# A gated MLP after linear attention on one core: a shorter reciprocal root, whole normalisation groups on GpSimd, and a new static instruction order

## Chip, core and metric

One core of a Trainium2 chip runs the whole program. The metric is device time in microseconds (us) of one execution, the median over several.

## The reference, cut to what matters

Linear attention with degree-2 sketched features, then a gated MLP whose gate mixes along the sequence (B=4, H=4, S=1088, D=32, r=8, d_ff=1024):

```python
phi = lambda x: outer(S1 @ x, S2 @ x)              # 8 x 8 = 64 features a head
x = (phi(q) @ (phi(k).T @ v)) / (phi(q) @ sum(phi(k)) + 1e-6)
h = gelu_tanh(x @ w_in);  u, v = h[..., :512], h[..., 512:]
v_n = (v - mean(v)) / sqrt(var(v) + 1e-6) * g_ln   # over the 512 columns
v_s = w_sg @ v_n + b_sg                            # 1088 x 1088 along the sequence
out = x + (u * v_s) @ w_out
```

`S1`, `S2`, `w_in` and `w_out` reach the chip as float64 words.

## The kernel before, in words

The sequence is cut into NT = 9 tiles of 128 rows and, along the free side, into chunks CH of 420, 420 and 248 columns. All work is a list of 1,839 steps (`add`, `step`), each with an engine, and `ORDER` (line 42) is a fixed permutation of them, written out as numbers: every engine (PE, V = VectorE/DVE, A = ScalarE/ACT, G = GpSimd/POOL, SP = the DMA-issuing queue) runs its own steps strictly in that order, and waits on semaphores for steps of others. PSUM buffers and scratch tiles are handed out along the same order: three `ps` buffers, two `pz`, three `po`.

Batch 0 alone is laid out for a short start. SP issues the loads (`first_loads`, line 434): `s` (the sketches), `k0` and `k1` (two parts of the keys), `win1`, `q0` to `q2`, `v0`, `v1`, the mixing weights `w0` to `w8`. `split64` (line 453) turns float64 words into a high and a low single-precision part in steps numbered 0 to 6, then `hi`, `l1`, `l2`; for names in `ONA` with more than 16 columns steps 2 and 4 run on A. The sketch `s` gives `sk` (line 505) and, on A, the expanded sketches `sab` (line 517). PE then runs `pk0` (key features, L526), `q2_0` (query features, L604), `k2_0` (keys by values, L534), `q3_0` (L581), a transpose `tr` (L598) and nine `pv0` (the gate half of `w_in`, L633 to L635). Each `pv0` tile passes A (`gelu`, L650), V (`bn`, bn_stats) or A (`bn`, a squared sum, L653), and a normalisation: group of tiles 0-1 on V (`norm 0`: `Gate.first` and `Gate.rest`, L294 to L311), tiles 2-5 and 6-8 on G after a `first` of three V instructions (`first 2`, `first 6`; `rest_g`, L316 to L330). The roots are a bit trick for the start value and two refinement steps. Then `v3` applies scale and shift (A, L333, or V, L666), and `part` (L673, L674) splits tiles into `ar` high and low, the stationary operands of the sequence mixing: `z0` (L695 to L699) and the columns of L1258 to L1262.

Meanwhile A rounds the mixing weights (`whi`, L668) and G makes their low parts (`w_lo`, L712); `HOLD` keeps G's pieces 12 and 15 of these behind `norm 0` and `norm 2`, the former by a small copy (L731). V converts `wi0` and `wo`; the last of those conversions (`staging`) frees the memory in which the later `gt`, `u`, `gh`, `gl` tiles lie, so no `u` (L764) of batch 0 can be written before it. The attention of batch 1 (k features L941, L267; `K2` L534; query product L996, then PE L1003) and the sums of weight blocks that batches 1 to 3 use (`combine`, L896 to L906, through HBM) run beside it.

Batches 1 to 3 do their mixing in seven instead of eight block products (`pair`); their normalisation groups are tiles 0-4 and 5-8 (GROUPS), each with `first` on V (line 1056) and `rest_g` on G (line 1057). Instructions marked `port` on G get a wait on the last V step marked `port`.

Of the kernel before, what the change touches and what calls it, by code (L numbers as in the profile page):

```python
# [1378 lines left out]
```

## Time and profile before

| | us |
|---|---|
| median of 3 runs (range) | 324.22 (323.77 to 325.99) |
| the profiled execution, whole | 322.75 |
| its span, first to last instruction | 320.9 |
| PE busy in the span | 309.9 |
| DVE / ACT / POOL busy | 256.0 / 207.5 / 49.3 |

The profiled execution is 1.85 us longer than its span and 1.47 us below the median of the runs. A PE that is called busy has matmuls in flight; an idle stretch of it is a wait.

### The profile page before, as it was taken

To read this page: it belongs to the slowest core of one execution; us is meant where nothing else is said; L and a number is where in the kernel's file an instruction comes from. 1 tells how busy PE (TensorE), PEld (TensorE's weight loads), DVE (VectorE), ACT (ScalarE), POOL (GpSimd) and SP (SyncE) were. 2 spreads that over 40 slices of the span, in tenths; PEclk is the share of its full clock that TensorE was granted. 3 is DMA by queue.
4 is the path that set the end of the run, shared out by engine and by line. 5 is a ranking of instruction groups with operands and counts; after the bars stand their busy time and mean duration, and the time that the engine had idled before them with its cause. 6 is when DMAs were issued, how large, how long until landed. Compare 5 with 4: busy or idle time off the path is not lost.

```text
span 320.9 us, 6428 instructions
## 1 busy us (share of the span) xinstructions
PE 309.9 (97%) x2318; PEld 285.0 (89%) x2318; DVE 256.0 (80%) x561; ACT 207.5 (65%) x491; POOL 49.3 (15%) x126
## 2 busy tenths in 40 slices
PE   5998899999999999999999999999999999999995
PEld 5865889898788998899899999988999999999995
DVE  4878999998988799977865787897976586796574
ACT  4679990766799987375959846358789833432421
POOL 0187792000003400000003300000032100000000
PEclk9799999999999999999999999999999999999999
DMA  7948885754778868973486279840534037205802
GB/s 223 389 132 273 274 274 134 236 164 132 216 211 258 235 195 222 349 217 73 125 254 222 73 165 244 253 133 4 156 117 160 0 110 229 109 29 175 283 0 69
DMA packets 42126, 57.08 MB, mean 178 GB/s; under 512 B 4080, under 2 KB 37104, under 8 KB 42096
## 3 DMA queue, kind: packets, MB, share of 16 engines
q1 hardware_dynamic: 41952, 56.64, 58.3%
q8 instruction: 18, 0.29, 0.4%
q14 instruction: 12, 0.10, 0.1%
q10 hardware_dynamic: 144, 0.05, 0.1%
HBM read 46.73 MB, written 9.95 MB: 177 GB/s over the span
## 4 chain that ended last, share of the span: by engine, by line
PE 78%; DVE 8%; ACT 5%; DMA 5%; issue 2%; SPq 1%; DVEq 0%; ACTq 0%
PE pz L843 15%; PE pz L844 15%; PE pz L845 15%; PE po L795 2%; PE po L796 2%; PE po L797 2%; PE ps L758 2%; PE pz L854 2%; PE ps L759 2%; PE ps L760 2%; PE pz L855 2%; PE ps L1037 2%; PE ps L1039 2%; PE ps L1038 2%; PE ps L1003 2%
## 5 line engine op out<-in xcount | busy, mean ns | idle before, releaser
L843 PE MATMUL pz<-w_h,ar 128*128 128x420 f32 (+1 forms) x288 | 94.0, 326 | 0.0
L844 PE MATMUL pz<-w_h,ar 128*128 128x420 f32 (+1 forms) x288 | 93.2, 324 | 0.0
L845 PE MATMUL pz<-w_l,ar 128*128 128x420 f32 (+1 forms) x288 | 93.0, 323 | 0.0
L843 PEld LDWEIGHTS pz<-w_h,ar 128*128 128x128 f32 x288 | 54.1, 188 | 4.1 <-issue 1.4
L844 PEld LDWEIGHTS pz<-w_h,ar 128*128 128x128 f32 x288 | 54.1, 188 | 1.1
L845 PEld LDWEIGHTS pz<-w_l,ar 128*128 128x128 f32 x288 | 54.2, 188 | 0.6
L818 ACT CAST ar<-vn 128x512 fp32r<-128x512 f32 x40 | 24.4, 619 | 23.4 <-PE pz L845 19.2
L789 ACT CAST gh<-gt 128x420 fp32r<-128x420 f32 (+1 forms) x47 | 23.2, 495 | 20.5 <-DVE gt L788 16.2
L819 DVE TENSOR_TENSOR ar<-vn,ar 128x512 fp32r<-128x512 f32 x40 | 27.3, 684 | 9.1 <-ACT ar L818 8.9
L790 DVE TENSOR_TENSOR gl<-gt,gh 128x420 fp32r<-128x420 f32 (+1 forms) x47 | 24.8, 532 | 12.1 <-ACT gh L789 11.7
L764 ACT ACTIVATE u<-ps 128x420 f32<-128x420 f32 (+1 forms) x48 | 21.9, 468 | 12.9 <-PE ps L760 11.3
L788 DVE TENSOR_TENSOR gt<-gt,u 128x420 f32<-128x420 f32 (+1 forms) x47 | 24.8, 532 | 4.1 <-ACT u L764 3.7
L333 ACT ACTIVATE vn<-vn,st 128x512 f32<-128x512 f32 x33 | 25.1, 807 | 0.0
L712 POOL TENSOR_TENSOR w_l<-w_f,w_h 128x420 fp32r<-128x420 f32 (+1 forms) x21 | 21.4, 1045 | 2.2 <-ACT w_h L668 1.2
L1049 ACT ACTIVATE kp<-vn,st 128x512 bf16<-128x512 f32 x27 | 19.4, 720 | 0.5
L774 DVE SCALAR_TENSOR_TENSOR gt<-pz,g_col,b_bc 128x420 f32<-128x420 f32 (+1 forms) x31 | 17.8, 573 | 1.6 <-PE pz L855 1.3
L1046 ACT ACTIVATE vn<-ps 128x512 f32<-128x512 f32 x27 | 16.0, 595 | 3.1 <-PE ps L1039 2.7
L316 POOL TENSOR_TENSOR st<-st 128x4 f32<-128x4 f32 (+2 forms) x8 | 2.5, 314 | 97.9 <-DVE st L298 97.0
L758 PE MATMUL ps<-x_h,win_h 128*128 128x420 f32 (+1 forms) x48 | 16.0, 332 | 0.0
L760 PE MATMUL ps<-x_l,win_h 128*128 128x420 f32 (+1 forms) x48 | 15.7, 328 | 0.0
L759 PE MATMUL ps<-x_h,win_l 128*128 128x420 f32 (+1 forms) x48 | 15.7, 328 | 0.0
L795 PE MATMUL po<-gh,wout_h 128*128 128x420 f32 (+1 forms) x47 | 15.7, 333 | 0.0
(260 smaller groups left out, 709.0 us busy)
## 6 DMA issues: line engine op xcount, KB each, us to landing
w_h<-td SPq DMA_DIRECT2D x26, 420.0 KB
w_l<-td SPq DMA_DIRECT2D x52, 210.0 KB
td<-tmp SPq DMA_DIRECT2D x16, 315.0 KB
w_f<-in_w SPq DMA_DIRECT2D x9, 544.0 KB
eb<-dq SPq DMA_DIRECT2D x6, 364.0 KB
ea<-dq SPq DMA_DIRECT2D x12, 182.0 KB
vn<-in_k SPq DMA_DIRECT2D x3, 576.0 KB
tmp<-in_w SPq DMA_DIRECT2D x16, 105.0 KB
```

Source lines behind the costliest of these rows:

```text
L333: return A.activation(self.vn(t), self.vn(t), AF.Identity, bias=self.nm[:, t : t + 1], scale=self.rs[:, t : t + 1])
L758: mm(o, lhsT=win_h[:, ws], rhs=xh[:, cs], start=True, stop=False)
L759: mm(o, lhsT=win_l[:, ws], rhs=xh[:, cs], start=False, stop=False)
L760: mm(o, lhsT=win_h[:, ws], rhs=xl[:, cs], start=False, stop=True)
L788: add("V", dv(cw), lambda: V.tensor_mul(gt(k)[:, :cw], gt(k)[:, :cw], utt[plan.got[u]][:, :cw]), r=[u], w=[k], free=[u], port=1)
L789: add("A", ac(cw), lambda: A.copy(ght[plan.got[h]][:, :cw], gt(k)[:, :cw]), r=[k], take={h: "gh"})
L790: add("V", dv(cw), lambda: V.tensor_sub(glt[plan.got[l]][:, :cw], gt(k)[:, :cw], f32(ght[plan.got[h]][:, :cw])), r=[h, k], take={l: "gl"}, ...
L818: add("A", ac(n), lambda: A.copy(dst[:, 0], q()), r=r, w=[key])
L819: add("V", dv(n), lambda: V.tensor_sub(dst[:, 1], q(), f32(dst[:, 0])), r=r, w=[key], port=1)
L843: mm(o, lhsT=ar[e][:, 0, t], rhs=wh, start=first, stop=False, skip_group_check=True)
L844: mm(o, lhsT=ar[e][:, 1, t], rhs=wh, start=False, stop=False, skip_group_check=True)
L845: mm(o, lhsT=ar[e][:, 0, t], rhs=wl, start=False, stop=last, skip_group_check=True)
```

## The change

- **Roots.** `first` makes the start value with two instructions instead of three, one bit trick with a factor -0.5 on the integer view. `rest` (V, used by group 0-1 alone) evaluates a cubic in place of two refinement steps: 12 V instructions become 10.
- **GpSimd from the variance on.** For the groups that G normalises, `first` runs on G too: 3 V instructions become 2 G instructions, in front of `rest_g`. This touches `norm 2`, `norm 6` and six groups of batches 1 to 3.
- **Conversions.** `s` joins `ONA`: its steps 2 and 4 (128x16) go from V to A. `wi1 l1` (128x512, a subtraction) goes from V to G.
- **HOLD** is empty, the copy is gone. The list has 1,830 steps. `KG`, `QG` and `FILL` are empty or zero and add nothing.
- **ORDER** is another permutation. Its starts, decoded by engine (`b1` is batch 1; `w_lo n` the n-th piece):

```
SP  before  k0 s win1 k1 q0 v0 q1 v1 w0 ident q2 w1 w2 ...
    after   s k0 k1 q0 win1 v1 v0 w0 q1 ident q2 (b1 q) w1 w2 w3 win0 ...
PE  before  pk0.0 pk0.2 pk0.1 q2_0.0.0 q2_0.0.1 q2_0.1.0 k2_0 (9) q2_0.1.1 q3_0.0 q2_0.2.0 q3_0.1 ...
    after   pk0.0 pk0.1 q2_0.0.0 pk0.2 q2_0.0.1 k2_0 (9) q2_0.1.0 q2_0.1.1 q3_0.0 q2_0.2.0 q3_0.1 ...
    before  ... pv0.7, b1: Q2.0 Q2.1 K1 K1 K1 K2, z0 tiles 0-1, L1260 ... z0.5, b1: Q2.2 K2 K2
    after   ... pv0.7, b1: K1 Q2.1 K1 K1, z0 tiles 0-1, b1: K2 Q2.2 K2 K2, L1260 ...
A   before  wi1.2 sab(4) kb0 sab(4) ...  whi1 x1 x1 ...  gelu7 mean6 skq bn6 ... bn7 ... bn8 v3.1
    after   s.2 s.4 sab(6) kb0 kb0 sab(1,3) qa1 kb0 wi1.2 sab(1,1) ...  skq whi1 x1 x1 ...
            gelu6 bn6 gelu7 (b1 Q2 copies) v3.1 a0.h kb kb bn7 bn8 kb v3.3
V   before  ... bn0 first2 norm0 v3.0 features(3) first6 a0.l ... L996 of b1 at place 86, 114, 139
    after   ... bn0 norm0 v3.0 (2 of combine) a0.l features(3) ... L996 of b1 at place 73, 110, 133
G   before  wi1.l2 w_lo 0-11 norm2 copy norm6 w_lo 12-20 wi0.l2
    after   wi1.l1 w_lo 0 wi1.l2 w_lo 1-10 norm2 w_lo 11 norm6 w_lo 12-20 wi0.l2
```

The diff, cut to its core:

```diff
+ROOT = (1.0, 0.99999624, 1.49998809, 2.51218104, 4.40140684)
-ONA = ("wi1", "wi0", "wo")
-HOLD = {12:0,15:2}
+ONA = ("s", "wi1", "wi0", "wo")
+HOLD = {}
+LOWG = ("wi1",)
...
-        def first(self, t0, n, summed=True):
+        def first(self, t0, n, summed=True, by=None):
-            V.tensor_scalar(yi, ve.bitcast(I32), 1, None, op0=ALU.logical_shift_right)
-            return V.tensor_scalar(yi, yi, -1.0, float(0x9EF759DF), op0=ALU.mult, op1=ALU.add)
+            return by.tensor_scalar(y.bitcast(I32), ve.bitcast(I32), -0.5, float(0x1EF759DF), op0=ALU.mult, op1=ALU.add)
...
             V.tensor_mul(h, h, ve)
-            V.tensor_scalar(p, h, 1.5, 2.5, op0=ALU.mult, op1=ALU.add)
-            V.tensor_mul(p, p, h)
-            V.scalar_tensor_tensor(y, p, 1.875, y, op0=ALU.add, op1=ALU.mult)
-            V.tensor_mul(h, y, y)
-            V.tensor_mul(h, h, ve)
-            V.scalar_tensor_tensor(self.rs[:, ts], h, 1.5, y, op0=ALU.add, op1=ALU.mult)
+            V.tensor_scalar(h, h, 0.5, None, op0=ALU.add)
+            V.scalar_tensor_tensor(p, h, ROOT[3] / ROOT[4], h, op0=ALU.add, op1=ALU.mult)
+            for c in ROOT[2:0:-1]:
+                V.scalar_tensor_tensor(p, p, c / ROOT[4], h, op0=ALU.add, op1=ALU.mult)
+            V.scalar_tensor_tensor(self.rs[:, ts], p, ROOT[0] / ROOT[4], y, op0=ALU.add, op1=ALU.mult)
...
-        onA = n > 16 and name in ONA
+        onA = name in ONA
...
-        step((name, "l1"), "V", 0.61, lambda: V.tensor_sub(t(), t(), f32(hi)), [(name, "hi"), (name, 5)], port=1)
+        step((name, "l1"), "G" if name in LOWG else "V", 0.61, lambda: (G if name in LOWG else V).tensor_sub(t(), t(), f32(hi)), [(name, "hi"), (name, 5)], port=1)
...
-            step(("first", t0), "V", 0.49, lambda t0=t0, n=n, s=summed: g.first(t0, n, s), bn, port=1)
-            step(("norm", t0), "G", 4.1, lambda t0=t0, n=n, s=summed: g.rest_g(t0, n, s), [("first", t0)])
+            step(("norm", t0), "G", 4.1, lambda t0=t0, n=n, s=summed: (g.first(t0, n, s, G), g.rest_g(t0, n, s))[1], bn)
...
-            add("V", 0.55, lambda t0=t0, n=n: g.first(t0, n), r=mk, w=[nk], port=1)
-            add("G", 3.5, lambda t0=t0, n=n: g.rest_g(t0, n), r=mk, w=[nk])
+            add("G", 3.9, lambda t0=t0, n=n: (g.first(t0, n, by=G), g.rest_g(t0, n))[1], r=mk, w=[nk])
```

## Rows read from the trace of the kernel before

**Rows 1.** Page, the span in 40 slices of 8.02 us: PE busy, granted clock (tenths)
```profile
PE   5998899999999999999999999999999999999995
PEclk9799999999999999999999999999999999999999
```

**Rows 2.** Stretches: length, busy PE, PEld, DVE, ACT, POOL; PEclk, DMA, GB/s
```profile
0.00:4.20 4.20, 3.25 (x28) 3.06 (x28) 1.14 (x12) 1.49 (x2) 0.43 (x6) 1.00 0.46 125
4.20:7.40 3.20, 0.57 (x12) 0.43 (x12) 1.78 (x7) 1.24 (x4) 0.00 (x0) 1.00 0.98 325
7.40:11.30 3.90, 3.90 (x33) 3.60 (x35) 3.80 (x9) 2.76 (x11) 0.00 (x0) 0.56 1.05 384
28.00:34.17 6.17, 3.44 (x70) 2.68 (x68) 5.55 (x26) 6.10 (x22) 3.78 (x16) 1.00 0.75 255
43.20:84.20 41.00, 41.00 (x260) 38.38 (x258) 38.40 (x72) 23.35 (x55) 7.13 (x8) 1.00 0.61 177
86.20:315.90 229.70, 229.66 (x1613) 215.87 (x1609) 179.47 (x380) 149.00 (x358) 18.08 (x68) 1.00 0.55 163
```

**Rows 3.** What PE waited for: us in total, times, longest
```profile
PE ps L526 <- DMA k<-in_k: 1.8, 1, 1.8
PE ps L534 <- DVE st L294: 1.4, 1, 1.4
...
PE ps L1003 <- DVE r L996: 0.6, 1, 0.6
PE ps L976 <- DVE vn L267: 0.5, 1, 0.5
```

**Rows 4.** Timeline of SP, the first loads: start, us, what
```profile
1.18 0.41 SPq L435 DMA_DIRECT2D sg_sraw<-in_s  x1
1.64 0.42 SPq L444 DMA_DIRECT2D sg_wraw_wi<-in_w_in  x1
2.11 0.43 SPq L437 DMA_DIRECT2D k<-in_k  x1
```

**Rows 5.** Timeline of DVE: sketch conversion, and the first normalisation group
```profile
3.33 0.17 DVE L470 TENSOR_SCALAR sp_s_t<-sg_sraw 128x16 int32<-128x16 int32 x1 [2.04 <-DMA sg_sraw<-in_s]
...
28.68 0.14 DVE L296 TENSOR_SCALAR st<-st 128x4 f32<-128x4 f32 x1
...
29.13 0.16 DVE L296 TENSOR_SCALAR st<-st 128x2 f32<-128x2 f32 x1
...
31.33 0.16 DVE L311 SCALAR_TENSOR_TENSOR st<-st 128x2 f32<-128x2 f32 x1
```

**Rows 6.** Timeline of POOL: a 128x512 conversion, first and last of group 2-5
```profile
14.50 1.27 POOL L493 TENSOR_TENSOR win_l<-sp_wi_t,sp_wi_e 128x512 fp32r<-128x512 f32 x1 [13.54 <-DVE sp_wi_t L492]
...
29.30 0.20 POOL L316 TENSOR_TENSOR st<-st 128x4 f32<-128x4 f32 x1 [0.88 <-DVE st L296]
...
32.71 0.20 POOL L330 TENSOR_TENSOR st<-st 128x4 f32<-128x4 f32 x1
```

**Rows 7.** Timeline, PE and ACT: first k2_0, q3_0, v3 and z0
```profile
12.20 2.32 PE L534 MATMUL pz<-sg_vx,vn 128*64 128x64 f32 x72
...
15.30 0.92 PE L581 MATMUL pz<-sg_kvx,vn 128*64 128x66 f32 x24
...
32.32 0.80 ACT L333 ACTIVATE vn<-vn,st 128x512 f32<-128x512 f32 x1
...
34.17 0.38 PE L697 MATMUL po<-w_h,ar 128*128 128x248 f32 x1
```

**Rows 8.** Timeline of DVE: one subtraction without, and one beside, POOL's w_lo
```profile
35.29 0.68 DVE L674 TENSOR_TENSOR ar<-vn,ar 128x512 fp32r<-128x512 f32 x1
...
42.27 1.57 DVE L674 TENSOR_TENSOR ar<-vn,ar 128x512 fp32r<-128x512 f32 x1
```

**Rows 9.** Chain that ended last: end of the staging, and batch 1's last L996
```profile
62.64 0.47 DVE wout_l L493
...
84.43 0.82 DVE r L996
```

More of the change, by code (lines that the diff above doesn't have):

```diff
@@ L32 @@
 WARM = 14
+ROOT = (1.0, 0.99999624, 1.49998809, 2.51218104, 4.40140684)
 LOWS = 7
-ONA = ("wi1", "wi0", "wo")
-HOLD = {12:0,15:2}
+ONA = ("s", "wi1", "wi0", "wo")
+HOLD = {}
 V30 = "VAVAVAAAA"
 STAT = "VVA"
+LOWG = ("wi1",)
+KG = ()
+QG = ()
+FILL = 0
 NORM = "VGG"
@@ L262, in tile_kernel, with features @@
         mm(pst[i % 3][:64, :64], lhsT=kp0[:, :64], rhs=kp0[:, :64], start=True, stop=True)
-    def features(out, a, b):
+    def features(out, a, b, by=None):
         sh = [P, 2, 2, R, R]
-        return V.tensor_tensor(
+        return (by or V).tensor_tensor(
             out.rearrange("t (p h i j) -> t p h i j", p=2, h=2, i=R),
-            a[:, :64].rearrange("t (p x h i) -> t p x h i", p=2, x=2, h=2)[:, :, 0].unsqueeze(4).broadcast_to(sh),
+            (a.rearrange("t (p h i) -> t p h i", p=2, h=2) if by else a[:, :64].rearrange("t (p x h i) -> t p x h i", p=2, x=2, h=2)[:, :, 0]).unsqueeze(4).broadcast_to(sh),
             b.rearrange("t (p h j) -> t p h j", p=2, h=2).unsqueeze(3).broadcast_to(sh),
@@ L288, in vn @@
             return vn[:, t, :DG]
-        def first(self, t0, n, summed=True):
+        def first(self, t0, n, summed=True, by=None):
             ve, y = (x[:, :n] for x in self.ch[t0][:2])
-            yi, ts = y.bitcast(I32), slice(t0, t0 + n)
+            ts, f = slice(t0, t0 + n), -0.5 if by is G else -0.5 / ROOT[4] ** 2
+            by = by or V
             if summed:
-                V.tensor_scalar(ve, self.mv[:, ts, 1], -0.5 / DG, -0.5 * EPS, op0=ALU.mult, op1=ALU.add)
+                by.tensor_scalar(ve, self.mv[:, ts, 1], f / DG, f * EPS, op0=ALU.mult, op1=ALU.add)
             else:
-                V.tensor_scalar(ve, self.mv[:, ts, 1], EPS, -0.5, op0=ALU.add, op1=ALU.mult)
-            V.tensor_scalar(yi, ve.bitcast(I32), 1, None, op0=ALU.logical_shift_right)
-            return V.tensor_scalar(yi, yi, -1.0, float(0x9EF759DF), op0=ALU.mult, op1=ALU.add)
+                by.tensor_scalar(ve, self.mv[:, ts, 1], EPS, f, op0=ALU.add, op1=ALU.mult)
+            return by.tensor_scalar(y.bitcast(I32), ve.bitcast(I32), -0.5, float(0x1EF759DF), op0=ALU.mult, op1=ALU.add)
         def rest(self, t0, n, summed=True):
@@ L412, in tile_kernel @@
     sab, kvx = staged("sab", [P, 2, 2, P], "sab"), staged("kvx", [P, 2, 2, D + 1], "kvx")
-    kb0 = staged("kb0", [P, 3, 32], None)
+    kb0, ka0 = staged("kb0", [P, 3, 32], None), staged("ka0", [P, 3, 32], None)
     ident = staged("ident", [P, P], "ident")
@@ L554, in tile_kernel @@
         ), [pk], r=[pk])
+        if c in KG:
+            step(("ka0", c), "A", 0.14, lambda c=c: A.copy(
+                ka0(c).rearrange("q t (p c) -> q t p c", p=2),
+                ps(("pk0", c))[:, : 3 * 64].rearrange("q (t p x c) -> q t p x c", t=3, p=2, x=2)[:, :, :, 0],
+            ), [pk], r=[pk], free=[pk])
         for i in range(3):
@@ L557, in tile_kernel @@
             kk = [("vn", 2, t, x) for x in range(2)]
-            step(("kp0", t), "V", 0.34, lambda c=c, i=i, t=t: features(vn[:, t, 512:768], ps(("pk0", c))[:, 64 * i : 64 * i + 64], kb0(c)[:, i]),
-               [("kb0", c)], r=[pk], w=kk, free=[pk] if i == 2 else [])
+            if c in KG:
+                step(("kp0", t), "G", 0.7, lambda c=c, i=i, t=t: features(vn[:, t, 512:768], ka0(c)[:, i], kb0(c)[:, i], G), [("kb0", c), ("ka0", c)], w=kk, port=1)
+            else:
+                step(("kp0", t), "V", 0.34, lambda c=c, i=i, t=t: features(vn[:, t, 512:768], ps(("pk0", c))[:, 64 * i : 64 * i + 64], kb0(c)[:, i]),
+                   [("kb0", c)], r=[pk], w=kk, free=[pk] if i == 2 else [])
             step(("k2_0", t), "PE", 0.45, lambda t=t: k2_0(t), ["v0", "v1", "vx1"], r=kk + [("vx", 0), ("vx", 1)], w=[("psn", 1)])
@@ L618, in tile_kernel @@
             step(("qa", j), "A", 0.38, lambda j=j: A.copy(et[j % 4], pab0(j, 0)), [("q2_0", c, 0)] + [("qp", j - 4)] * (j >= 4), r=[pa, "ea", "eb"], free=fa)
-            step(("qp", j), "V", 0.475, lambda j=j, c=c, p=p: V.tensor_mul(qp0(c, p), pab0(j, 1), et[j % 4]), [("qa", j), ("q2_0", c, 1)],
-               r=[pb, "ea", "eb"], free=fb)
+            if j in QG:
+                step(("qb", j), "A", 0.38, lambda j=j, c=c, p=p: A.copy(qp0(c, p), pab0(j, 1)), [("q2_0", c, 1)], r=[pb, "ea", "eb"], free=fb)
+                step(("qp", j), "G", 0.95, lambda j=j, c=c, p=p: G.tensor_mul(qp0(c, p), qp0(c, p), et[j % 4]), [("qa", j), ("qb", j)], r=["ea", "eb"], port=1)
+            else:
+                step(("qp", j), "V", 0.475, lambda j=j, c=c, p=p: V.tensor_mul(qp0(c, p), pab0(j, 1), et[j % 4]), [("qa", j), ("q2_0", c, 1)],
+                   r=[pb, "ea", "eb"], free=fb)
         if c == 0:
@@ L666, in tile_kernel @@
                 step(("v3", t), "V", 0.45, lambda t=t: V.tensor_scalar(g.vn(t), g.vn(t), g.rs[:, t : t + 1], g.nm[:, t : t + 1], op0=ALU.mult, op1=ALU.add), [("norm", t0)], w=vk[t], port=1)
+    for i in range(FILL):
+        k = ("fill", i)
+        if i < FILL // 2:
+            step(k, "PE", 0.2, lambda k=k: (mm(ps(k)[:64, :64], lhsT=sk[:, :64], rhs=sk[:, :64], start=True, stop=True),
+                                            mm(ps(k)[:64, :64], lhsT=sk[:, :64], rhs=sk[:, :64], start=True, stop=True)), ["sk"], take={k: "ps"}, free=[k])
+        else:
+            step(k, "PE", 0.17, lambda k=k: mm(ps(k)[:, : 3 * P], lhsT=win_h[:, DG : DG + P], rhs=xh0[:, : 3 * P], start=True, stop=True), [("wi1", "hi")], r=[("x", 0, 0)], take={k: "ps"}, free=[k])
     for t in range(NT):
```

184 rows, old and new, of the table ORDER are left out of this document.

## The prediction

> **What bounds the kernel now.** I read the slices of the page first: PE is busy 9 tenths or more in every slice from the sixth to the last but one, and its clock is full but for the first two slices [rows 1]. The stretches say it sharper: from 86.20 to 315.90 us PE is busy 229.66 of 229.70 us, and from 43.20 to 84.20 all 41.00 [rows 2]. The change removes no matmul, so neither stretch can get shorter; what can move is when PE comes to them. Before 43 us PE loses time in three places. From 4.20 to 7.40 it is busy only 0.57 of 3.20 us, and in the 3.90 us behind that its clock is 0.56 on average, that is mostly the 1.2 GHz level, while it works without pause [rows 2]. From 28.00 to 34.17 it is busy 3.44 of 6.17 us [rows 2]. The waits name the causes: 1.8 us for the load of k1 (L526), 1.4 us put down to an instruction of the normalisation (L534), 0.5 us for key features of batch 1 (L976), and later 0.6 us for the query product L996 (L1003) [rows 3].
>
> The chain that ended last tells the second thing: between 34 and 85 us it runs through DVE, ACT and loads, not PE, through the end of the staging at 63.1 us (62.64 + 0.47) and through L996 at 84.43 [rows 9]. So PE's lead over the old run is worth only as much as DVE keeps pace: DVE is busy 38.40 of the 41.00 us from 43.20 on [rows 2].
>
> **The loads and the start.** SP issues a load each 0.46 us; `s` goes at 1.18, `win1` at 1.64, `k1` at 2.11 [rows 4]. DVE starts on `s` at 3.33 [rows 5]; with `s` issued first I take 0.46 us less, 2.87. `win1` is 512 columns of 8 bytes on 128 partitions, 0.52 MB, and stands ahead of k1 (0.39 MB). Bytes moved are 0.525 MB by 4.20 us (4.20 x 125) and 325 GB/s behind that [rows 2]. k0, s, win1 and k1 are 1.13 MB, reached at 6.06 us; k1 released PE 1.8 us into a wait that ended at 7.4, so a load counts as landed some 1.3 us behind its bytes. In the new order k1 ends at 0.61 MB: 4.45 + 1.3 = 5.8 us. q0 (0.20 MB) follows at 6.4, win1 (1.33 MB in all) at 8.0 instead of 6.1, and v1 and v0 (1.92 MB, at 384 GB/s past 7.40) at 9.6.
>
> PE then does `pk0.1` at 5.8, `q2_0.0.0` at 6.4, `pk0.2`; `q2_0.0.1` needs sab(1,1), which stands on ACT behind the `wi1` step that waits for win1, so at about 8.9. The nine `k2_0`, which begin at 12.20 before [rows 7], can begin at 9.9; DVE paces them (its last key features end near 11.5 behind four steps of `wi1`), so they end at about 12.1. They took 2.32 us [rows 7], to 14.52, so the lead is 2.4 us. `q2_0.1.0`, before them in the old list, now stands behind them: two query steps of 0.9 us each and `q3_0.0` at 13.9 instead of 15.30 [rows 7]. **Lead 1.4 us.** From there to the `pv0` PE works without waits in either list, and ACT's `skq`, moved ahead of `whi1`, costs ACT 0.24 us off PE's path.
>
> The conversion edits themselves are small here. Two of the eight instructions on `s` leave DVE: independent ones come about 0.1 us apart, so 0.2 us at most less; ACT's two run beside DVE's first two, and I keep 0.1. If ACT is late by the whole of a 0.2 us step each, it is a loss of 0.3. `wi1 l1` on GpSimd: no subtraction of that shape on it is in the trace, the nearest is the sum `l2` at 1.27 us [rows 6]. `l1` and `l2` then end near 16.0 us, and the first `pv0` that needs them comes at 19.5: cost nothing, cover 3.5 us.
>
> **The normalisation.** `norm 0` starts on DVE at 29.13, after `first 2` from 28.68, and its last result starts at 31.33 [rows 5]. Removed are the 0.45 us of `first 2` and two of twelve instructions, 2 x 0.2 = 0.4. With the lead of 1.4 `norm 0` ends at 31.5 - 1.4 - 0.45 - 0.4 = 29.25 us. The first `v3` on ACT was at 32.32 [rows 7] behind two squared sums (`bn7`, `bn8`), which the new list puts behind it: it runs at 29.3. Then `a0` high and low as before (34.17 - 32.32 = 1.85): z0 at 31.15, **lead 3.0**. PE has 2.0 us of z0 on two tiles, then three K2 and one Q2 of batch 1 (2.5 us in the old trace's pace), which fill the wait for `ar(0)`; that one is ready only at about 35.1, since the squared sums now stand ahead of it. At 35.6 PE comes to L1260, before at 36.26; but the old list had 1.8 us of K2 and Q2 and a 0.6 us wait still to come. 0.65 + 1.8 + 0.6 = 3.05 us: the lead stays 3.0.
>
> On GpSimd group 2-5 was 29.30 to 32.91, 13 instructions, 0.28 each [rows 6]. It takes 2 more, +0.56 us, but no longer queues behind DVE (0.62 from 28.68 to 29.30 [rows 5, 6]) and starts after `w_lo 10` near 26.6: done by 31, nobody waits. What would be late next is group 6-8: the squared sum of tile 8 ends near 32, it ends near 37, and its `v3` stands on ACT at 37.
>
> **What is given back.** The end of the staging lets ACT write the first `u`, which frees the `ps` buffer for PE's third unit. DVE leaves out up to there 0.7 (`l1`), 0.95 (`first 2`, `first 6`), 0.4 and 0.2; with the front's 1.4 (in which 0.9 of these are used) and about 0.45 of work that the list puts ahead, I get 63.1 - 2.0 = 61.1. PE, 3.0 ahead, would want that buffer at 61.5, gets it about 62: 0.5 us lost. At L1003 the old wait of 0.6 (0.8 against the pace of its neighbours) goes, if L996 comes as early as the list has it: 3.4 us of DVE work less stand ahead. I take 0.5 of it. Sum at 86 us: 3.0 - 0.5 + 0.5 = 3.0.
>
> In batches 1 to 3, six groups: DVE loses 3 instructions each, GpSimd gains 2 (0.56 us). DVE is off PE's path there; a group that ends later moves six `v3` and `ar` by 0.56 - 0.5 = nothing. For new waits in 230 us without one I put 0.2. The end (315.90 to 320.9) has the same steps.
>
> **Sum.** -3.0 + 0.2 = -2.8 us. Against the profiled execution, 322.75 - 2.8 = 319.95; against the median of the runs, 1.47 higher, **321.4 us**, 0.9% less.
>
> One rule speaks against `l1` on GpSimd. The row: DVE's 128x512 subtraction took 0.68 us alone and 1.57 beside POOL's `w_lo` [rows 8]. The Trainium skill, "SBUF — State Buffer", section "Who interferes with whom", says that DVE and GpSimd share one port pair as an exclusive lock, and that a DVE instruction with two SBUF inputs is blocked for as long as a GpSimd instruction that reads SBUF holds it. By that rule the sum would lose up to 1.27 us where `l1` runs beside `wi1` step 6; by my sum nothing. The trace agrees that the price exists (0.89 us on that row).
>
> **The rivals.** (a) *Nothing is given back, and the clock holds.* PE pauses less before 9 us, no half-speed stretch follows, the buffer wait does not come, L1003 waits for nothing: 3.0 + 0.3 + 0.2, and up to 1.7 us (3.4 us at half speed: (1 - 0.56) x 2 x 3.90 [rows 2]) where PE and not DVE paced: -3.5 to -5. From the median 320.7 to 319.2. For it: the old pause of 2.6 us before the slow stretch [rows 2]. Against it: DVE at 94% behind 43 us. (b) *Given back.* `l1` blocks step 6, `kv0` is 0.9 late, the lead shrinks to 0.5; or PE still falls to half speed and loses 1.2; or the staging is early by 1.0 only and PE waits 1.5 us at its third unit. Each leaves -0.5 to -1.8: about 323. For it: the contention rows, and that ACT's pause for win1 leaves PE idle near 8 us. (c) *A wait in the late stretch.* The six groups on GpSimd, now behind two more instructions, come after PE wants their `ar`. Decides: the new list's slack in front of each group; at 1.0 us late each, 6.0 us, -2.8 + 6.0 = +3.2: 327.4. The break-even with before is 0.47 us a group. Against it: the old list had no wait there at all [rows 2], and the groups' last tiles come 1 to 2 us earlier in PE's order. (d) *The changes do nothing*: k1 lands no earlier because the queue, not the bytes ahead, sets it. Then only the normalisation's 1.6 us is left: 322.6.
>
> **How the numbers follow.** Forecast (-1.8 to -3.2) 0.38, (a) 0.30, (b) and (d) 0.20, (c) 0.12, of which 0.02 stays near nothing. About 1% (3.2 us) is what a measurement of this kernel can tell from no change. The forecast's own range is 321.0 to 322.4, just inside 1%; with 0.04 of it beyond, faster is 0.34, slower 0.10, same 0.56. The range of 8 in 10 goes from 318.9, past (a), to 324.4, past (b) and (d), and leaves (c) out.
>
> **What would show it.** Right: PE's wait on k1 under 0.8 us and the clock full from 7.4 to 11.3; q3_0 first at 13.9, z0 at 31.2; no wait at L976 near 41; the staging at 61; PE at its long stretch 3 us earlier and busy all through. Wrong: k1 landing past 6.5; `wi1` step 6 over 1.2 us; a wait of PE at its third unit over 1 us; any wait of PE above 0.3 us behind 86 us.

## The result, and the profile after

The changed kernel takes 328.35 us (median of four executions, 327.19 to 329.74) against 324.06 us: a ratio of 1.0107, interval 1.0060 to 1.0153. It is 1.1% slower. The prediction was 321.4 us, range 318.9 to 324.4.

| us | before | after |
|---|---|---|
| the profiled execution, whole | 322.75 | 329.74 |
| its span | 320.9 | 327.6 |
| PE busy in the span | 309.9 | 313.0 |
| DVE / ACT / POOL busy | 256.0 / 207.5 / 49.3 | 249.4 / 208.6 / 56.2 |
| first `pv0` on PE | 20.88 | 19.13 |
| first `z0` on PE | 34.17 | 31.19 |
| `z0` to PE's last result | 283.98 | 293.57 |

DVE is busy 6.6 us less, and PE reaches `z0` 2.98 us earlier, where the sum said 3.0. Behind `z0` the kernel loses 9.6 us. A part of that is work that changed places: one `K2` of batch 1 (24 matmuls, 33.33 to 34.17 us) stands ahead of `z0` in the old list and behind it in the new. From the first `pv0`, which has it behind it in both, PE takes 305.63 us to its last result, where it took 297.27: 8.4 us lost. And the profiled execution is the slowest of the four, though its front ran at the full level and no run's first `pv0` came more than 0.05 us earlier; the two fastest had a span of 325.3 us, so behind `z0` they lost at least some 2 us less. The page of the changed kernel, 40 slices of 8.19 us, shows where:

```profile
PE   7988994999999999999999999999999999999995
DVE  4888755989997888987685778887775695875765
PEclk9999997899999999999999999999999999999998
```

The seventh slice (49.1 to 57.3 us) has PE at 4 tenths, where before there was 9, and the granted clock falls in it and the next, where before it was full [rows 1]. The stretches (length, then busy PE, PEld, DVE, ACT, POOL; PEclk, DMA, GB/s) give the front and that place:

```profile
4.20:7.40 3.20, 2.77 (x40) 1.84 (x40) 1.80 (x7) 2.43 (x11) 0.00 (x0) 1.00 1.01 329
7.40:11.30 3.90, 2.33 (x54) 1.79 (x56) 3.63 (x10) 3.14 (x7) 0.00 (x0) 1.00 1.03 373
...
50.00:56.00 6.00, 2.27 (x19) 1.10 (x20) 2.96 (x4) 1.41 (x4) 0.00 (x0) 0.72 0.64 165
56.00:60.00 4.00, 4.00 (x14) 3.81 (x14) 3.97 (x8) 2.76 (x6) 0.00 (x0) 0.56 0.96 331
```

In the front PE is busy 2.77 us of the 3.20 in which it had 0.57, and the clock behind is 1.00, where it was 0.56 [rows 2]. The price is paid from 50 us on. PE's waits (us in total, times, longest) put a name to it:

```profile
PE ps L1025 <- DVE r L1018: 4.1, 1, 4.1
PE po L616 <- ACT sg_sab L521: 1.6, 1, 1.6
PE ps L268 <- POOL kp L266: 0.9, 1, 0.9
PE po L719 <- ACT ar L695: 0.7, 1, 0.7
PE ps L1059 <- ACT vn L1068: 0.6, 1, 0.6
```

L1025 and L1018 are L1003 and L996 of the kernel before, the query product of batch 1: DVE multiplies its two factors, loaded from HBM into `ea` and `eb`, into `r`, and PE takes `r` from there. It comes in three chunks, and this is the first. The kernel before, its first and its third:

```profile
56.76 0.90 DVE L996 TENSOR_TENSOR r<-ea,eb 128x728 f32<-128x728 f32 x1
59.01 0.84 PE L1003 MATMUL ps<-r,kp 64*32 64x364 f32 x16
...
85.39 0.84 PE L1003 MATMUL ps<-r,kp 64*32 64x360 f32 x16 [0.65 <-DVE r L996]
```

The first had no wait; the 0.6 us of [rows 3] lie at the third. The new list brings the first forward on PE, from 59.01 to 49.61 us, and the wait comes there. Back along the timelines of the changed kernel (start, length, what, idle time before it). DVE, then PE:

```profile
45.03 0.90 DVE L701 TENSOR_TENSOR rs<-vn,rs 64x128 fp32r<-64x128 f32 x2
52.76 0.92 DVE L1018 TENSOR_TENSOR r<-ea,eb 128x728 f32<-128x728 f32 x1 [6.82 <-DMA eb<-dq]
...
53.73 1.47 PE L1025 MATMUL ps<-r,kp 64*32 64x364 f32 x16 [4.12 <-DVE r L1018]
...
58.87 0.55 PE L1283 MATMUL pz<-w_h,ar 128*128 128x420 f32 x1
59.22 0.48 PE L1281 MATMUL pz<-w_h,ar 128*128 128x420 f32 x1
59.54 0.35 PE L1283 MATMUL pz<-w_h,ar 128*128 128x420 f32 x1
```

DVE comes to L1018 at 45.93 us and stands there 6.82 us for a load; its list is strict, so everything behind it stands too. PE stands 4.12 us, and its matmuls take 0.55 us each instead of 0.35 until 59.48: the granted clock is 0.50, the 1.2 GHz level, from 52.66 us, within that wait, to there. ACT waits 6.54 us for `g_col` at the same place. Why the load is late stands on SP's timeline and GpSimd's:

```profile
30.43 11.62 SPq L433 DMA_DIRECT2D w_f<-in_w  x3
42.11 0.45 SPq L1003 DMA_DIRECT2D dq<-ab  x1
42.73 1.38 SPq L1014 DMA_DIRECT2D ea<-dq  x2
44.15 0.44 SPq L928 DMA_DIRECT2D td<-tmp  x1
44.64 0.57 SPq L1011 DMA_DIRECT2D eb<-dq  x1
45.25 0.67 SPq L451 DMA_DIRECT2D g_col<-in_g  x1
...
38.31 10.29 POOL L734 TENSOR_TENSOR w_l<-w_f,w_h 128x420 fp32r<-128x420 f32 x9
```

The last of the three loads in the first row is the mixing weight `w7`. It was issued at 41.73, after 5.1 us for GpSimd's `w_lo` and 4.8 for ACT's rounding (waits of SP at L433); before, at 34.65. A load of `w` needs a buffer of a former tile, and buffers are handed out along `ORDER`, to the loads and to the first piece of `w_lo` of each tile. In the old list `w7` gets the one that piece 11 of `w_lo` frees. In the new list piece 15 (tile 5) stands ahead of `w7` too, as piece 12 (tile 4) does in both; it takes one more buffer, and `w7` gets the one that piece 14 frees, on a GpSimd that is busy with group 6-8 until 38.35. The two `ea` loads, `td`, `eb` and `g_col` stand behind `w7` on SP and go out when it goes. So the chain is: GpSimd's normalisation, its `w_lo` pieces, the buffer, `w7` on SP, `eb`, DVE, PE. Of PE's waits from 84 to 320 us, three are listed, 1.4 us together.

### The profile page after: what moved, and what is told of

Read it like the earlier page. It is cut to its first block, busy times and chain, and to the rows that moved or that the text cites. A ratio compares the mean times of both kernels' runs of the same rounds, so it can differ in the third digit from the quotient of the medians.

```text
span 327.6 us, 6423 instructions
## 1 busy us (share of the span) xinstructions
PE 313.0 (96%) x2318; PEld 284.5 (87%) x2318; DVE 249.4 (76%) x532; ACT 208.6 (64%) x493; POOL 56.2 (17%) x142
## 4 chain that ended last, share of the span: by engine, by line
PE 77%; ACT 7%; DVE 6%; DMA 5%; issue 2%; SPq 1%; POOL 1%; POOLq 0%; DVEq 0%; ACTq 0%
PE pz L865 13%; PE pz L866 13%; PE pz L867 13%; DMA eb<-dq 2%; PE ps L1025 2%; PE ps L780 2%; PE po L817 2%; PE po L819 2%; PE po L818 2%; PE ps L781 2%; PE ps L782 2%; PE ps L1059 2%; PE pz L876 2%; DMA sg_wraw_wi<-in_w_in 2%; PE ps L1061 2%
## 5 line engine op out<-in xcount | busy, mean ns | idle before, releaser
L786 ACT ACTIVATE u<-ps 128x420 f32<-128x420 f32 (+1 forms) x48 | 22.0, 467 | 13.9 <-PE ps L782 10.5
L337 ACT ACTIVATE vn<-vn,st 128x512 f32<-128x512 f32 x33 | 25.8, 808 | 0.6 <-POOL st L331 0.5
L300 POOL TENSOR_SCALAR st<-st 128x5 f32<-128x5 f32 (+2 forms) x7 | 1.4, 196 | 140.6 <-ACT kp L1071 138.8
```

The lines of the kernel that those rows point to most:

```text
L337: return A.activation(self.vn(t), self.vn(t), AF.Identity, bias=self.nm[:, t : t + 1], scale=self.rs[:, t : t + 1])
```

## The experiments

Theory: the buffer of `w7`, through SP and DVE, costs the time, and PE's clock behind the wait comes on top. Rivals: the edits cost it (GpSimd's groups, the conversions); the front costs it in most executions; or the clock alone does. Each run stands beside runs of the kernel before on the same chip (medians 324.81, 324.29, 324.43, 324.64 and 323.64 us for the five sets).

**The edits alone** (the changed code, in the old order without the nine steps that are gone), and **the list alone** (the old code in the new order):

```diff
-    1, 13, 11, 12, 14, 16, 15, 17, 18, 45, 49, 50, 47, 51, 0, 2, 46, 42, 43, 53,
+    2, 1, 11, 12, 13, 14, 15, 10, 16, 21, 17, 18, 45, 46, 47, 42, 43, 3, 19, 53,
...
```

> The changed kernel's edits (roots, GpSimd groups, conversions, no HOLD) with the list of the kernel before, the removed steps left out of it. Theory A (the list did it, the edits are harmless or a small gain): no wait at L1025, PE's wait on k1 near 1.8 us as before, group 0-1 normalised about 0.85 us earlier than before, span 319.0 to 320.9 (before 320.9). Theory C (the edits cost: GpSimd's groups are later, and PE's mixing waits for them): new PE waits of 0.3 us and more behind 86 us or at 43 to 60 us, span 322 or more.

> The edits of the kernel before with the new list, the removed steps put back ahead of their successors (the three first steps of a group on DVE, HOLD's copy, l1 of wi1 and the steps of s on DVE). Theory A: the load of w7 still stands ahead of ea and eb on SP, the wait at L1025 is 3 to 6 us, the clock falls behind it, span 326.5 to 330. Theory C (the edits do it): the wait at L1025 is under 1 us and the span is 322 or less.

The edits alone: 324.22 us, ratio 0.9994 (0.9967 to 1.0021), nothing. The list alone: 340.96 us, 1.0471 (1.0403 to 1.0538). PE's waits of the latter, in its slowest execution:

```profile
PE ps L1003 <- DVE r L996: 5.4, 1, 5.4
PE ps L976 <- DVE vn L267: 2.3, 1, 2.3
PE po L604 <- ACT sg_sab L517: 2.1, 1, 2.1
PE pz L843 <- ACT vn L333: 1.6, 1, 1.6
```

The wait on the query product is there without any of the edits: the list makes it. The list also does not stand without the edits for which it was found.

**The loads ahead of `w7`, and PE kept at work.** The first puts the loads of `ea` and `eb` (steps 411, 412) ahead of the load of `w7` (36); the second gives PE 19 matmuls, whose results nobody reads, in place of the wait.

```diff
-551, 39, 207, 187, 262, 211, 35, 405, 36, 172, ... 183, 411, 115, ... 554, 412, 184,
+551, 39, 207, 187, 262, 211, 35, 405, 411, 412, 36, 172, ... 183, 115, ... 554, 184,
...
-            def q3(pd=pd, cw=cw):
+            def q3(pd=pd, cw=cw, dummies=19 * (b == 1 and ci == 0)):
+                for i in range(dummies):
+                    mm(ps(pd[i % 2])[:, :420], lhsT=w_h[:, 0, :P], rhs=w_h[:, 0, :420], start=True, stop=True)
```

> Changed kernel with two moves in the list: on SP, the two loads of ea and the load of eb for the first chunk of batch 1 stand ahead of the load of w7 instead of behind it. Theory A (the query product L1018, and PE's L1025 behind it, are late because SP stands on the load of w7 until GpSimd's piece 14 is done at 41.7 us): the ea loads go out at about 36.6 us (42.73 in the changed kernel), when the key products L538 are done, eb by 38.2, L1018 starts when DVE is free at about 46 (52.76), PE has no wait above 0.5 us at L1025, the clock stays full, and the span is 327.6 - 4.1 (the wait) - 2.9 (53.73 to 59.48 at half speed) = 320.6 us. Theory B (the 8 us from the issue of eb to its use are the transfer itself, or PE's list is simply too early): L1018 starts no earlier than 50, a wait above 1.5 us stays, span 323 or more.

> The changed kernel with 19 matmuls of 128x420 that nobody reads, put on PE directly ahead of the first query product L1025, so that PE works while it would wait (about 3.6 us of the 4.1). Theory D (the half-speed stretch from 52.66 to 59.48 comes of PE's pause, and costs as much again as most of the wait): the wait at L1025 shrinks to about 0.5 us, the granted clock is full from 44 to 60, and the span is 327.6 - 2.9 = 324.7. Rival (the clock falls there for another reason, or the half speed costs nothing because other engines pace): the clock is below 0.8 in 54 to 59 as before, or it is full and the span is still 327.

With the loads moved, PE's wait at L1025 is gone, and `z0` to the end takes 289.6 us instead of 293.6. The median is 329.16 all the same: in the profiled execution the front ran at the 1.2 GHz level (0.50) from 9.32 to 16.14, and the first `pv0` came at 22.86, 3.7 us later than in the changed kernel's. One of the four executions took 323.43. So that run shows the repair and hides it behind a second cause.

With PE kept at work the granted clock is full from 6.02 us on and the wait is gone, and the time is 331.86 (1.0202, 1.0111 to 1.0293), no better. `z0` to the end takes 294.31 us in its profile, where it took 293.57. PE waits elsewhere instead (the second line is the front's):

```profile
PE ps L998 <- DMA qld<-in_q: 1.4, 1, 1.4
PE po L616 <- ACT sg_sab L521: 1.1, 1, 1.1
PE pz L865 <- DVE gt L796: 1.1, 2, 0.9
...
PE ps L998 <- ACT t4a L924: 0.9, 1, 0.9
```

The clock is a symptom: what the faster PE wins back it waits for DVE, ACT and SP again. DVE still stood 5.43 us at L1018 there. The 19 matmuls end at 53.18, 0.9 us after DVE's result, so up to that much of it they cost themselves.

**The buffer.** Pieces 12 to 16 of `w_lo` (steps 240 to 244) are written behind the load of `w7`; every engine's own order is unchanged, only the buffers are handed out differently. In the second run only pieces 15 and 16 are.

```diff
-    33, 148, 205, 170, 178, 402, 240, 446, 447, 114, 403, 179, 404, 256, 259, 241, 242, 34, 171, 243,
-    244, 544, 163, ...     211, 35, 405, 36, 172, 245,
+    33, 148, 205, 170, 178, 402, 446, 447, 114, 403, 179, 404, 256, 259, 34, 171, 544, 163, ...
+    211, 35, 405, 36, 240, 241, 242, 243, 244, 172, 245,
```

> The changed kernel with five steps of GpSimd (pieces 12 to 16 of w_lo) written behind the load of w7 in the list, with no other step of GpSimd or SP passed: every engine runs the same steps in the same order as in the changed kernel, but the buffers are handed out in another order, and w7 gets the one that piece 8 leaves free instead of the one that piece 14 leaves. Theory A (SP's stand on the load of w7 is the cause, through ea and eb and through the store td behind it): w7 is issued near 32 us (41.73), ea near 37 (42.73), td near 41.2 (44.15), eb near 41.7 (44.64); L1018 starts by 47 (52.76); no wait of PE at L1025 above 0.5 us and none at L719 for w_h; the span is 327.6 - 4.1 - 2.9 - 0.5 = 320.1 us, or less. Theory B (behind 50 us a second chain of sums, stores and loads on DVE and SP holds PE, as the waits at L998 and L865 in the two runs before suggest, whatever is won at L1025): the wait at L1025 goes, PE waits 1.5 us or more in 55 to 75 us, and the span is 323 or more.

> As e5_buffer, but only pieces 15 and 16 of w_lo are written behind the load of w7: w7 gets the buffer that piece 11 leaves free (near 31.4 us), and pieces 12 to 14 keep the wait on DVE that they have in the changed kernel (in e5_buffer they stood 2.4 us more, to 41.69, and DVE then waited 2.7 us for the last piece at L741). Theory A (DVE, not PE, sets the pace from 45 us on, and the changed kernel lost what DVE lost: it stood 6.8 us at L1018, to 52.76): GpSimd's pieces end near 49, L741 starts near 49.3 (51.98 in e5_buffer), and the span, counted from the first z0 (325.1 - 32.1 = 293.0 in e5_buffer), shrinks by about 2.5 to 290.5 us. Theory B (PE's own waits at L998 and L780 are set by loads and not by DVE): counted so it stays within 1 us of 293.

326.59 us (1.0070, 1.0043 to 1.0097) and 326.41 (1.0053, 1.0025 to 1.0081). `z0` to the end falls from 293.6 to 290.1 and 288.5 us. SP's timeline in the second run:

```profile
31.28 1.50 SPq L433 DMA_DIRECT2D w_f<-in_w  x3
32.88 0.48 SPq L1003 DMA_DIRECT2D dq<-ab  x1
37.21 1.65 SPq L1014 DMA_DIRECT2D ea<-dq  x2
42.01 0.38 SPq L928 DMA_DIRECT2D td<-tmp  x1
42.44 0.57 SPq L1011 DMA_DIRECT2D eb<-dq  x1
```

`w7` goes out 9 us earlier, and DVE waits 0.18 us at L1018, not 6.82. `eb` goes out only 2.2 us earlier (42.44 for 44.64); the rest is that from issue to use it took 4.5 us instead of 8.1, now that `w7` and `ea` no longer go out in the 3 us ahead of it. No run separates these two parts. In the first run GpSimd has to start piece 12 late in turn, and DVE stands 2.7 us at L741 for it; in the second 1.66. The cause of the large wait is settled: it goes when the loads are moved and when the buffer is, and it comes with the list alone. Its price is less certain. In the profiled executions 5.1 of the 9.6 us behind `z0` come back, in the medians 0.5% (1.0107 to 1.0053, with intervals that overlap). And 4.5 us stay, with PE's waits near 65 us. The end of the staging on DVE, the first `u` on ACT behind it, and PE, in the second run:

```profile
63.90 0.69 DVE L497 TENSOR_TENSOR wout_l<-sp_wo_t,sp_wo_e 128x512 fp32r<-128x512 f32 x1
64.71 0.93 ACT L786 ACTIVATE u<-ps 128x420 f32<-128x420 f32 x2 [1.04 <-DVE wout_l L497]
65.28 0.46 PE L780 MATMUL ps<-x_h,win_h 128*128 128x420 f32 x1 [0.99 <-ACT u L786]
67.03 0.47 PE L865 MATMUL pz<-w_h,ar 128*128 128x420 f32 x1 [0.90 <-DVE gt L796]
```

The staging ends at 64.59 us, later than the 63.1 of before, and PE waits 0.99 us for what hangs on it.

**Is it a load that waits on SP?** In the first buffer run PE also waited 1.36 us near 60 us for `qld` of batch 2 (L998). On top of the second run, that load goes ahead of a load of `tmp` that waits on SP.

```diff
-118, 120, 123, 537, 560, 419, 557, 420, 562, 195, 896, 561, 563,
+118, 120, 123, 537, 560, 419, 896, 557, 420, 562, 195, 561, 563,
```

> The kernel of e9_buffer2 with one load moved on SP: qld of batch 2 (L993) ahead of the load of tmp that waits 9 us for DVE's t4a (L926). Theory B (loads behind a waiting one on SP set PE's wait at L998 near 60 us): the wait of 1.4 us at L998 goes and the span is 1 to 1.5 us less than e9_buffer2's, counted from z0. Theory A (DVE sets the pace there): the wait goes, but others of the same size take its place within 10 us, and counted from z0 the span is within 0.5 us of e9_buffer2's.

From the first `pv0` to the end it took 300.25 us, against 300.57 without the edit, and the median is 325.39 (1.0025, 0.9999 to 1.0050). But the run decides nothing: the second buffer run had no wait near 60 us to begin with (its waits behind `z0` are at 65, 67, 100 and 110 us), so the edit took none away. That DVE sets the pace there is argued from its load and from the staging's end above, not shown by this run.

**The front.** The new list up to the last `pv0`, or up to the load of `w7` with the buffers of the first buffer run, and the old one behind it:

```diff
-    150, 151, 152, 158, 159, 407, 153, 154, 129, 126, 382, 397, 238, 130, 155, 131, 545, 426, 427, 145,
+    150, 151, 152, 158, 159, 407, 153, 154, 426, 544, 382, 129, 384, 238, 239, 126, 145, 155, 386, 34,
...
```

> The changed kernel's edits with the new list through the last pv0 (about 28 us), and from there on the order of the list before. It asks whether the front's lead holds under the old rest. Theory A (the front's lead and the normalisation are worth what the steps say where no new wait comes): z0 near 31.5 us (34.17 before), PE 2 us ahead into its long stretch, of which the old list's DVE keeps about half: span 318.5 to 320. Theory B (DVE, SP and the loads set the pace between 34 and 85 us, not PE): the lead is gone by 86 us, in waits of PE of 1 us or more between 40 and 86, span 320.5 to 322.

> As e7_front, but with the new list up to the load of w7 (about 32 us on SP, the third z0 tile on PE), with the buffers of e5_buffer, and from there on the old order. Theory A: as for e7_front, with the new normalisation order as well: z0 at 31.2, span 318 to 319.5. Theory B: span 320.5 or more, with waits of PE between 40 and 86 us.

324.19 us (0.9989, 0.9960 to 1.0017; 321.48 to 327.78) and 328.88 (1.0121, 1.0080 to 1.0161). The new front followed by the old order gives nothing. The second tells where the rest may lie: from the first `pv0` to the end its profile has 302.11 us with the old order behind `w7`, the first buffer run 302.15 with the new, and the kernel with the old order from the last `pv0` on 298.78. So the loss that stays does not need the new order behind the load of `w7`; the stretch between the last `pv0` and there, or the joint of the two lists, can make it. No run separates them. Four query-feature matmuls tell why it can differ from one execution to the next. The changed kernel, then the one with the new front only:

```profile
5.94 0.92 PE L616 MATMUL po<-r,sg_sab 64*128 64x384 f32 x4
6.78 0.57 PE L530 MATMUL ps<-sk,k 128*64 128x64 f32 x12
8.96 0.59 PE L616 MATMUL po<-r,sg_sab 64*128 64x384 f32 x1 [1.61 <-ACT sg_sab L521]
...
6.26 1.65 PE L616 MATMUL po<-r,sg_sab 64*128 64x384 f32 x4
7.85 0.91 PE L530 MATMUL ps<-sk,k 128*64 128x64 f32 x12
9.88 1.00 PE L616 MATMUL po<-r,sg_sab 64*128 64x384 f32 x1 [1.13 <-ACT sg_sab L521]
```

The list is the same up to there, and the same instructions take 0.92 or 1.65 us; the granted clock has no record in the second case before 13.4 us, so the level is read from the durations. In eleven profiled executions of kernels with the new front and no idle matmuls in it, five ran it at the full level (`k2_0` in 2.32 us) and six wholly or partly at half (3.14 to 4.11 us), to 16.7 us at the latest, and the first `pv0` came anywhere from 19.08 to 23.82 us. The old front gave 20.88 and, with the edits, 21.14. What the prediction took for a lead of 1.4 us is the good end of that spread.

**What disturbs it.** Two guesses: PE's pauses of 1 to 2.6 us between 5 and 10 us, or the later loads beside the first ones. Against the first, 14 idle 64x64 matmuls (nobody reads their results) ahead of the second query step, on the first buffer run; against the second, a memset on DVE that holds back the loads from `v1` on until 4.34 and 4.12 us, with the list of the second buffer run and with the new front only.

```diff
+        for _ in range(14 * (c == 0 and i == 1)):
+            mm(pab0(0, 1)[:64, :64], lhsT=kp0[:, :64], rhs=kp0[:, :64], start=True, stop=True)
...
-        step(n, "V", 0.15, lambda x=x: V.tensor_tensor(
+        step(n, "V", 0.15, lambda x=x: (V.tensor_tensor(
...
-        ), ["sk1"] if x else [("s", "whole")])
+        ), x and V.memset(vx()[:, NT + 1, :1], 0.0))[0], ["sk1"] if x else [("s", "whole")])
```

> The kernel of e5_buffer with 14 matmuls of 64x64 that nobody reads on PE ahead of the second query features (L616), where the changed kernel's PE waits 1.6 us for sab: PE works through that pause. Theory D (the runs of one program differ by some us because the clock falls to half behind the pause near 8 us in some executions and not in others): the granted clock is full from 7 to 20 us, and the times of the runs lie within 1 us of each other, at the lowest of e5_buffer's. Rival (the pause is too short to matter, or the spread comes from elsewhere): the runs spread by 2 us or more as in e1_sp (323.4 to 329.2).

> The kernel of e9_buffer2 with one small DVE instruction behind sk (a zero written into the place that the load of v1 fills), so that SP issues v1, v0, w0 and what follows only after about 4.3 us (3.06 in the changed kernel), and s, k0, k1, q0 and win1 have the DMA engines to themselves until then. Theory E (the new front's lead is a matter of chance: with eight loads under way k1, q0 and win1 land up to 2 us later in one execution than in the next, and PE's pause for sab at L616 lasts 1.1 to 2.3 us): win1 lands before 8 us, the waits at L616 sum to under 1 us, z0 starts at 31 us or sooner, and the times of the runs spread over less than 2 us. Rival (the spread comes from elsewhere, or v1 and v0 then come too late for the nine k2_0): waits at L538 before 12 us of 0.5 us and more, z0 at 31.5 or later, and the spread of e9_buffer2.

> The kernel of e7_front (new list to the last pv0, old order behind it; its runs lie from 321.5 to 327.8, median 324.2) with the held-back loads of e10_hold. Theory E: the runs keep to the lower half of that spread, median 321.5 to 322.5, below the kernel before. Rival: the median stays at 324 within 0.7, or rises.

The first took 329.86 us (1.0171): there PE paused 1.54 us for `q0`, ahead of the idle matmuls, and ran at half clock from 7.55 to 10.96, so it decides nothing. The held loads: 326.54 (1.0051) and 324.31 (0.9990, 0.9960 to 1.0020), as without; the second guess falls. In the latter's profiled execution the first `pv0` came at 19.08, and the span was 320.9, that of the kernel before to the tenth: 1.8 us ahead at `pv0`, nothing at the end.

So idle matmuls were put into all the pauses: 2 and 4 ahead of the key features, 8 and 20 ahead of the query steps; in the kernel with the new front only, in the kernel before (6 more at the start, 24 in the wait for k1), and in the second buffer run.

```diff
-WARM = 14
+WARM = 20
...
+    def idle(o, n):
+        for _ in range(n):
+            mm(o[:64, :64], lhsT=kp0[:, :64], rhs=kp0[:, :64], start=True, stop=True)
...
+        idle(ps(("pk0", c)), (2, 4, 0)[c])
...
+        idle(pab0(2 * c, i), ((8, 20)[i]) * (c == 0))
```

> The kernel of e7_front (new list to the last pv0, old order behind it) with matmuls of 64x64 that nobody reads in PE's three pauses at the start: 2 and 4 ahead of the key features, 8 ahead of the first query features, 20 ahead of the second. Theory F (PE's pauses between 5 and 10 us decide whether the granted clock is full there, and so whether the lead comes: first pv0 at 19.1 to 20.1 with it, 21.5 to 23.8 without): the granted clock is full from 5 or 6 us to 20, the first pv0 starts by 20 us, and the runs keep to the lower half of e7_front's 321.5 to 327.8: median 321.5 to 323. Rival (the clock at the start does not depend on what PE does there): some runs above 325, median 323.5 to 325.

> The kernel before with such matmuls in its two pauses: 6 more behind the 14 at the start, and 24 ahead of the key features that wait for k1 (4.2 to 7.4 us). Theory F: the clock is full through 7.9 to 11.3 (half before), the first pv0 starts 0.5 to 1 us earlier than 20.9, and the median is 0.3 to 1 us below the kernel before. Rival (DVE paces there, the half speed cost nothing): the clock is full, and the first pv0 and the median are within 0.3 us of before.

> The kernel of e9_buffer2 (the new list throughout, w7's buffer mended) with the idle matmuls of e13_fill_old. Theory F: first pv0 by 20 us, from there to the end 300.6 us as in e9_buffer2, e10_hold and e12_qld, so a span of 322.5 to 323.5 and a median of 324 to 325 (e9_buffer2 326.4). Rival: the median stays within 0.7 us of 326.4.

324.36 us (0.9986, 0.9970 to 1.0002), 323.98 (0.9979, 0.9953 to 1.0006) and 327.25 (1.0092, 1.0061 to 1.0122). In the profiled executions of the five kernels with the new front and filled pauses (these two and the three below), `k2_0` takes 2.32 or 2.37 us each time and the front runs at full rate: five of five, against five of eleven. That speaks for the pauses, but they are not shown as the cause, and cannot be the whole of it. In three of the six slow executions (the two fronts followed by the old order, and the held loads with the new list) the first 24 key-feature matmuls, from 4.2 us on and ahead of any of these pauses, already took 322 to 323 ns each on average, where two executions at the full level there have 229. And the longest pause, 2.58 us in the second buffer run, was followed by the full level. The first kernel's twelve executions lie within 1.6 us, against 6.3 without the idle matmuls; the kernel before, filled, still spreads over 4.0 us, so a part of the spread stays open. The matmuls themselves were too many:

```profile
8.43 0.57 PE L535 MATMUL ps<-sk,k 128*64 128x64 f32 x12
8.83 2.50 PE L529 MATMUL po<-kp 128*64 128x64 f32 x40
11.26 0.59 PE L622 MATMUL po<-r,sg_sab 64*128 64x384 f32 x1
```

They end at 11.3 us, where `sab` was ready at 10.1. So half as many; and the waits taken out of the lists instead: the last piece of `sab` ahead of `wi1` on ACT, three key features ahead of it on DVE, with 16 and then 6 idle matmuls ahead of the first `k2_0` in place of most of those ahead of the second query step.

```diff
-        idle(pab0(2 * c, i), ((8, 20)[i]) * (c == 0))
+        idle(pab0(2 * c, i), ((4, 10)[i]) * (c == 0))
...
-    54, 55, 3, 4, 61, 62, 57, 59, 10, 52, 77, 81, 6, 69, 70, 65, 63, 67, 5, 19,
-    21, 20, 48, 78, 56, 73, 22, 79, 29, 7, 58, 60, 23, 64, 80, 9, 71, 8, 75, 66,
+    54, 55, 3, 4, 61, 62, 57, 59, 10, 52, 77, 81, 6, 69, 70, 65, 63, 67, 5, 71,
+    73, 75, 19, 48, 21, 20, 78, 56, 22, 79, 29, 7, 58, 60, 23, 64, 80, 9, 8, 66,
```

> The kernel of e13_fill_old with the steps that wait for win1 moved behind the front's own: on ACT the last sab ahead of step 2 of wi1, on DVE the last three key features ahead of step 0 of wi1, and the idle matmuls moved from the second query features (4 left) to the first k2_0 (16). Theory F: nothing in the front waits for win1 any more, k2_0 starts when v0 and v1 have landed (about 9.5 us), the first pv0 starts at 19 to 19.5 in spite of a late win1, the median is at or below that of e13_fill_old, by up to 0.7. Rival (the chain through wi1 to the low part of w_in is then late for pv0): a wait at L650 or L651 of 0.5 us or more, and a median above e13_fill_old's.

> The kernel of e13_fill_old with fewer idle matmuls: 1 and 2 ahead of the key features (2 and 4), 4 ahead of the first query features (8), 10 ahead of the second (20). In e13_fill_old the 20 took 2.50 us and ended at 11.26, while sab was ready at 10.10, and the 8 took 1.14. Theory F: the clock stays full in most runs, the first pv0 starts 1 to 1.8 us earlier than in e13_fill_old (21.43), and the median is 322.5 to 323.4 (324.36), below the kernel before by 0.3 to 0.6%. Rival (with less work in the pauses the clock is lost again in some runs): a spread of 3 us or more, median 323.5 to 324.5.

> The kernel of e16_nosab with fewer idle matmuls: 1 and 2 ahead of the key features, 4 ahead of the first query features, none ahead of the second, 6 ahead of the first k2_0 (16, which took 2.02 us). Theory F: first pv0 at 19.3 to 20.3 (21.35), median 322.5 to 323.5 (324.83), below the kernel before. Rival as for e17_fill_less: a spread of 3 us or more, median 323.5 to 325.

324.83 (0.9996), 323.48 (0.9997, 0.9980 to 1.0014) and 323.67 us (1.0001, 0.9982 to 1.0019). In the profiled executions of the last two the first `pv0` came at 20.53 and 19.68, and the time from there was 298.25 and 300.83 us, where the kernel before takes 297.27. Earlier at `pv0`, later behind it: none of these versions is faster than the kernel before by more than its measurement is uncertain.

## Why the prediction was wrong

*The start, right.* k1 released PE at 5.35 (said 5.8), `q0` at 5.94 (6.4), `win1` was there at 7.98 (8.0). PE's pause for `sab` ended at 8.96 (8.9), `k2_0` ran from 9.81 to 12.13 (9.9 to 12.1), `q3_0` came at 13.55 (13.9), and the clock behind 7.4 us was full. PE's wait on k1 fell from 1.8 [rows 3] to 0.2 us.

*Its certainty, wrong.* These numbers are those of one execution, so that they fit is in part luck. The prediction had the half-speed front only in rival (b) at 1.2 us; in the runs the first `pv0` came up to 4.7 us later (23.82 against 19.13), there with a load of `q0` that PE waited 1.4 us for.

*The normalisation, nearly right.* `norm 0` ended at 29.57 (29.25), `z0` came at 31.19 (31.15). From the first `pv0` to `z0` it is 12.05 us against 13.29: 1.2 gained where 1.6 was said, and 12.05 or 12.06 again in nine other kernels with the new list. Some 0.8 of the 1.2 is the `K2` that now stands behind `z0`: PE comes to L1281 (L1260 before), behind that `K2`, at 36.38 us, where 35.6 was said. Group 2-5 on GpSimd was done at 29.84 (31), group 6-8 ran to 38.35 (37).

*"What is given back", wrong.* The step that failed is the sum from `z0` to 86 us, 3.0 - 0.5 + 0.5. It has a term for the buffer of PE's third unit and one for the old wait at L1003, and it puts a new wait at batch 1's first query product at nothing, without a reason. The old wait, the third product's, did go, as said: PE has none at L1025 behind 84 us. But the list also puts the first L996 13 places earlier in DVE's order and its product 9.4 us earlier on PE, and I counted only DVE's own work ahead of L996. Its inputs come by SP, behind `w7`, whose buffer now depends on another piece of GpSimd's work. The diff of the order showed that piece 15 had moved ahead of `w7`, and `HOLD`, emptied by the change, had held it behind `norm 2`; I named the cover of group 6-8's `v3` and not what is queued behind it on GpSimd. The wait is 6.8 us of DVE and 4.1 of PE, with PE at the half level for 6.8 us around its end. The second buffer run takes it away and gives 5.1 us of the profiled time back.

*The staging, wrong.* It was to end at 61.1 us (by the terms named there it is 60.8: 0.7 + 0.95 + 0.4 + 0.2 + 1.4 - 0.9 - 0.45 is 2.3, not 2.0). In the changed kernel it ended at 68.18, behind DVE's stand, and no unit of PE waited for it; with the buffer mended at 64.59, and there the wait at PE's third unit came, 0.99 us for the 0.5 said.

*The rest, 4.5 us behind `z0`.* The prediction did say that PE's lead is worth only as much as DVE keeps pace, yet let 3.0 of 3.0 us through. The runs contradict it: with the old order behind `pv0`, first `pv0` at 19.08, 20.53 or 21.64 us ended PE's work at 318.20, 318.78 or 320.42, against 20.88 and 318.15 before; the edits alone left DVE 251.6 us of work for 256.0 and brought nothing. In the repaired list PE's waits of 1.0, 0.9, 0.6, 0.5 and 0.4 us make 3.4, where the kernel before has 1.7 behind `z0`, and the `K2` that changed places is 0.8 more; the remaining 2 us are in no wait that is listed. Which engine's place in the list would have to change is open; no run put the first query product back to its old place on PE.

*The rivals.* (c) named a time of 327.4 us, near the measured one, by another mechanism: late groups on GpSimd behind 86 us at 1.0 us each. PE waited 1.4 us there up to 320 us, none of it for a group, so (c) is not what happened. (b) had the right kind, a wait that gives the lead back, at 1.5 us and in another place. (a) and (d) fell; k1 did land early.

*The port rule* that the prediction weighed: `wi1 l1` on GpSimd took 1.77 us in the changed kernel and 1.28 with the old order, above the 1.27 taken as the nearest row [rows 6], and hid as said. The Trainium skill, "SBUF — State Buffer", section "Who interferes with whom", says that a DVE instruction with two SBUF inputs contends with a GpSimd instruction that reads SBUF; the trace agrees with DVE's 128x630 subtraction, 1.28 us beside GpSimd's `w_lo` in the changed kernel and 0.82 us in the first buffer run, where GpSimd stood. The latter's 0.46 us lie ahead of DVE's stand of 6.82 us, which covers them.
